# SwiGLU's second products of two token groups: seven block products with a transposed output, woven into the first products, and another order of the groups

## The chip, the cores and the metric

The kernel runs on one core of a Trainium2 chip. The metric is the device time of one execution in microseconds (us). Engines: TensorE (PE; its weight loads are PEld), VectorE (DVE), ScalarE (ACT), GpSimd (POOL) and the sync engine (SP), which issues every DMA of this kernel.

## The reference

Linear attention, a mixture of experts and a SwiGLU block follow each other on 4 x 576 = 2304 tokens of 512 features. The part that the change touches is the last function:

```python
def _moe2_ref(x, w_gate, w_val, w_out, rms_g) -> np.ndarray:
    rms = np.sqrt(np.mean(x * x, axis=-1, keepdims=True) + 1e-06)
    xn = x / rms * rms_g
    g = xn @ w_gate
    silu = g * (1.0 / (1.0 + np.exp(-g)))
    val = xn @ w_val
    return (silu * val @ w_out).astype(np.float32)
```

Here x is 2304 x 512, w_gate and w_val are 512 x 1536, w_out is 1536 x 512. Ahead of it every token goes through all 8 experts (`h = relu(x @ w1[e])`, `h @ w2[e]`, weighted sum). The weights of SwiGLU arrive as 64-bit floats.

## The kernel before

**Tiling.** The tokens are cut into three groups of 512, 896 and 896 (GP = 256, 448, 448, two halves each). The code counts them g = 0, 1, 2; the text calls them the first, second and third group. For each group all experts run first, in units of 256 hidden features (32 units a group, NCH); SwiGLU follows in units of 256 of its 1536 hidden features (6 units a group, NC2). Units are numbered through: 0 to 95 experts, from NU = 96 on SwiGLU. A unit has an "h" part (first products and activation) and a "y" part (second product, added into an accumulator).

**Three matmuls for one.** Every float32 operand is split into a high half (a ScalarE copy) and a low half (a subtraction), and `mm3` (lines 104 to 107) makes three matmuls of each product: high by high, high by low, low by high.

**First products of the large groups.** `seven` (line 792) makes the product of a 2x2-block weight and a 2x2-block x in seven block products instead of eight. Its operands are sums of blocks: those of x are stored in DRAM by the steps of `sx_steps` and loaded into seven tiles by `sx_load` (line 738), those of the weights are prepared in DRAM (`prepare`, line 398) and loaded by `ws_load` (line 287). After each product, ScalarE copies or VectorE adds out of the PSUM banks b1, b2, b3 (lines 801 to 825); line 825 is on GpSimd. SwiGLU runs `seven` twice, for gate and value, so a unit has 14 products. After product i a hook runs what is due there (`task`).

**Second products.** `y_mm` (line 895) takes a tile of 128 tokens as the weights and streams the 512 output columns: 7 token tiles x 2 hidden halves x 3 matmuls in the large groups, 4 x 2 x 3 in the first. Line 1097 adds the tile to the accumulator, and in the last unit line 1103 stores it. Four PSUM banks ("y") take the tiles in turn.

**Output weights.** During the third group's experts the SwiGLU weights are decoded from 64 bits, one step of VectorE or GpSimd at a time (`decode`, `dec`). Gate and value weights go on to `prepare`; the output weights are stored as float32 (W32, lines 360 to 364), and each unit loads its part and splits it (`w2_load`, `w2_split`).

**Order.** Each engine works its instructions in the order in which they are written here, and so does the sync queue: a DMA that waits holds those behind it. `stretch` (line 1140) writes h of unit u ahead of y of unit u - 1. The third group's experts and SwiGLU of the first and second group form one stretch, SwiGLU of the third group another (lines 1146 to 1148). The RMS norm of a group (`norm_steps`: squares, scale, transposes, then storing the x blocks through two pairs of staging buffers) is spread over hooks: the second group's over its successor's experts, the third group's over the SwiGLU units of the other two (lines 1281 to 1286).

## Time and profile before

| | us |
|---|---|
| median of 3 runs (lowest, highest) | 2020.91 (2019.67, 2021.41) |
| profiled execution, its own time | 2020.03 |
| span in the profile | 2018.2 |
| TensorE busy | 1993.7 (99%) |
| VectorE, ScalarE, GpSimd busy | 1407.4, 782.8, 377.5 |
| mean granted clock of TensorE | 0.998 of full speed |

The profile is one execution. A busy time is the time in which an engine had an instruction running; matmuls overlap, so the distance from one start to the next tells what one costs. The SwiGLU stages lie, in us of the span: first group from 1582 to 1687 (with the last expert tiles), second to 1852, third to the end.

### The profile page before, as it was taken

To read this page: it belongs to the slowest core of one execution; us is meant where nothing else is said; L and a number is where in the kernel's file an instruction comes from. 1 tells how busy PE (TensorE), PEld (TensorE's weight loads), DVE (VectorE), ACT (ScalarE), POOL (GpSimd) and SP (SyncE) were. 2 spreads that over 40 slices of the span, in tenths; PEclk is the share of its full clock that TensorE was granted. 3 is DMA by queue.
4 is the path that set the end of the run, shared out by engine and by line. 5 is a ranking of instruction groups with operands and counts; after the bars stand their busy time and mean duration, and the time that the engine had idled before them with its cause. 6 is when DMAs were issued, how large, how long until landed. Compare 5 with 4: busy or idle time off the path is not lost.

```text
span 2018.2 us, 25789 instructions
## 1 busy us (share of the span) xinstructions
PE 1993.7 (99%) x9614; PEld 1715.4 (85%) x9614; DVE 1407.4 (70%) x2161; ACT 782.8 (39%) x1383; POOL 377.5 (19%) x342
## 2 busy tenths in 40 slices
PE   7999999999999999999999999999999999999999
PEld 5777888888888888888888888888888888888887
DVE  8885877776677777776658878878865446565555
ACT  5564333345343343443243333333332253433432
POOL 3320000032222222222022222222220000110100
PEclk9999999999999999999999999999999999999999
DMA  7543322354765555654768778778865647557542
GB/s 203 143 136 110 95 95 100 99 204 177 261 216 199 197 217 211 219 210 172 296 251 285 249 244 312 275 273 286 282 233 195 256 146 263 214 203 276 194 158 74
DMA packets 169853, 415.11 MB, mean 206 GB/s; under 512 B 32256, under 2 KB 81920, under 8 KB 169344
## 3 DMA queue, kind: packets, MB, share of 16 engines
q1 hardware_dynamic: 169728, 413.47, 58.7%
q8 instruction: 75, 1.23, 0.3%
q14 instruction: 50, 0.41, 0.1%
HBM read 281.69 MB, written 131.73 MB: 205 GB/s over the span
## 4 chain that ended last, share of the span: by engine, by line
PE 95%; DVE 3%; ACT 1%; issue 0%; DMA 0%; POOL 0%; DVEq 0%; POOLq 0%; ACTq 0%
PE py L105 13%; PE py L106 13%; PE py L107 13%; PE b_a L107 10%; PE b_a L106 10%; PE b_a L105 10%; PE ph_a L105 3%; PE ph_a L107 3%; PE ph_a L106 3%; PE po L105 2%; PE po L107 2%; PE po L106 2%; PE b_v L105 2%; PE b_v L107 2%; PE b_v L106 2%; PE px L634 1%
## 5 line engine op out<-in xcount | busy, mean ns | idle before, releaser
L105 PE MATMUL py<-w2h,hh 128*128 128x512 f32 x1152 | 452.6, 393 | 0.7 <-ACT lt L684 0.7
L106 PE MATMUL py<-w2l,hh 128*128 128x512 f32 x1152 | 449.0, 390 | 0.0
L107 PE MATMUL py<-w2h,hl 128*128 128x512 f32 x1152 | 448.6, 389 | 0.0
L801 ACT COPY u_a<-b_a 128x448 f32<-128x448 f32 x228 | 121.6, 533 | 692.8 <-PE b_a L107 692.6
L105 PEld LDWEIGHTS py<-w2h,hh 128*128 128x128 f32 x1152 | 216.3, 188 | 47.2 <-issue 1.5
L107 PEld LDWEIGHTS py<-w2h,hl 128*128 128x128 f32 x1152 | 216.3, 188 | 45.7
L106 PEld LDWEIGHTS py<-w2l,hh 128*128 128x128 f32 x1152 | 216.3, 188 | 43.0
L105 PE MATMUL b_a<-sT,wsh_a 128*128 128x448 f32 x608 | 220.0, 362 | 3.2 <-DVE c L815 2.1
L107 PE MATMUL b_a<-sT,wsl_a 128*128 128x448 f32 x608 | 220.6, 363 | 0.0
L106 PE MATMUL b_a<-sT,wsh_a 128*128 128x448 f32 x608 | 220.3, 362 | 0.0
L929 DVE SCALAR_TENSOR_TENSOR slot_a<-py,Pm,slot_a 128x512 f32<-128x512 f32 x217 | 162.6, 749 | 52.3 <-PE py L107 50.4
L929 DVE SCALAR_TENSOR_TENSOR slot_b<-py,Pm,slot_b 128x512 f32<-128x512 f32 x217 | 161.4, 746 | 23.6 <-PE py L107 22.5
L107 PE MATMUL b_a<-sB,wsl_a 128*128 128x448 f32 x456 | 165.7, 363 | 0.3 <-DMA wsl_a<-wdl_a 0.3
L106 PE MATMUL b_a<-sB,wsh_a 128*128 128x448 f32 x456 | 165.2, 362 | 0.0
L105 PE MATMUL b_a<-sB,wsh_a 128*128 128x448 f32 x456 | 165.2, 362 | 0.0
L102 DVE TENSOR_TENSOR w2l<-w2r,w2h 128x512 fp32r<-128x512 f32 x162 | 116.9, 722 | 43.5 <-ACT w2h L101 43.5
L863 DVE SCALAR_TENSOR_TENSOR hl<-c,hh 128x896 fp32r<-128x896 f32 x128 | 143.1, 1118 | 0.9 <-ACT hh L862 0.7
L825 POOL TENSOR_TENSOR c<-u_a,p_a 128x448 f32<-128x448 f32 x64 | 74.2, 1159 | 344.1 <-ACT u_a L801 344.0
L862 ACT ACTIVATE hh<-c 128x896 fp32r<-128x896 f32 x128 | 122.4, 956 | 28.1 <-POOL c L825 28.1
L247 POOL TENSOR_TENSOR sum<-w1r 128x256 f32<-128x256 f32 x32 | 23.8, 742 | 561.5 <-issue 438.1
L101 ACT CAST w2h<-w2r 128x512 fp32r<-128x512 f32 x162 | 97.1, 618 | 81.3 <-PE py L107 77.1
L105 PEld LDWEIGHTS b_a<-sT,wsh_a 128*128 128x128 f32 x608 | 113.7, 187 | 13.1 <-DVE c L815 3.7
(232 smaller groups left out, 3594.9 us busy)
## 6 DMA issues: line engine op xcount, KB each, us to landing
w2r<-in_moe_w_dram SPq DMA_DIRECT2D x96, 512.0 KB, 4.6
w1r<-in_moe_w_dram SPq DMA_DIRECT2D x64, 512.0 KB, 3.4
wsdh<-wsh_a SPq DMA_DIRECT2D x32, 896.0 KB, 6.4
wsdl<-wsl_a SPq DMA_DIRECT2D x32, 896.0 KB, 7.8
wsh_a<-wsdh SPq DMA_DIRECT2D x32, 896.0 KB, 6.8
wsl_a<-wsdl SPq DMA_DIRECT2D x32, 896.0 KB, 8.7
w2d<-w2l SPq DMA_DIRECT2D x32, 512.0 KB, 2.9
w2l<-w2d SPq DMA_DIRECT2D x32, 512.0 KB, 4.8
```

The source lines that it names most:

```text
L101: nc.scalar.copy(hi, src)
L102: (eng or nc.vector).tensor_tensor(lo, src, hi.bitcast(F32), op=ALU.subtract)
L105: nc.tensor.matmul(ps, lh, rh, start=first, stop=False, skip_group_check=True)
L106: nc.tensor.matmul(ps, lh, rl, start=False, stop=False, skip_group_check=True)
L107: nc.tensor.matmul(ps, ll, rh, start=False, stop=last, skip_group_check=True)
L247: nc.gpsimd.tensor_tensor(s1, a21, a22, op=ALU.add)
L634: nc.tensor.matmul(px[:, :H2], st["kv"], st["qT"][:, n], start=True, stop=True)
L801: nc.scalar.copy(tmp[n], bk[i])
L825: nc.gpsimd.tensor_tensor(c[:, 1, 1], tmp["u3"], tmp["p5"], op=ALU.add)
L862: nc.scalar.activation(th, src, AF.Relu)
L863: return lambda: nc.vector.scalar_tensor_tensor(tl, src, 0.0, th.bitcast(F32), op0=ALU.max, op1=ALU.subtract)
L929: nc.vector.scalar_tensor_tensor(a, py, pe, a, op0=ALU.mult, op1=ALU.add)
```

## The change

For the second and third group the second product is also made of seven block products: 2 hidden halves x 2 token halves by 2 hidden halves x 2 output halves. Now the output weights are the stationary operand (128 x 128) and 448 tokens stream, so that the result is transposed: 128 output features by 448 tokens. A unit has 14 tiles of three matmuls.

- `prepare_out` makes the seven blocks of the output weights in DRAM while the other weights are prepared; `wo_load` brings them in four loads a unit, in place of `w2_load` and `w2_split`. `dec` runs the second line of steps on two calls of three, not on every second. W32 is still stored, for the first group.
- `tail_steps` makes the seven hidden blocks (four GpSimd subtractions, seven splits) at the last two hooks of a unit and in the first tiles of the next.
- `y_steps` queues 14 tiles; `y_step` runs one after each block product of the following unit. Each of seven products has its own accumulator, kept over the six units. The first unit copies, later ones add: ten tiles on VectorE from PSUM, four by a ScalarE copy and a GpSimd addition (STAGED).
- `y_end` combines the seven accumulators by seven GpSimd additions; `y_out` turns 32 x 32 blocks on VectorE and stores 32 tokens a DMA.
- The order of SwiGLU becomes second, third, first group. The h parts of the twelve units of the large groups follow each other without y parts between; the last expert tiles come after the first of them.
- The third group's norm moves into five units of the second group, its eight block subtractions (`two`) from VectorE to GpSimd. The loads of the x blocks move to the last expert unit and to the last unit of the second group; the first group's x comes back at unit U0 - 1.

```diff
     LATE = 4
+    TURN2 = (1, 2, 0)
+    U0 = NU + 2 * NC2
     const = ctx.enter_context(tc.tile_pool(name="const", bufs=1))
     slots = ctx.enter_context(tc.tile_pool(name="slots", bufs=1))
...
             del RAW["b", u]
-            if u + 1 < ALL:
-                w2_load(u + 1)
+            n = U0 if u + 1 == NU else u + 1
+            if n < ALL:
+                w2_load(n)
     def ws_alloc(key):
...
@@ -358,10 +361,8 @@
         nc.gpsimd.tensor_tensor(r, r, a.bitcast(F32), op=ALU.add)
         dec_load()
         if kind == "o" and half:
-            r = DEC.pop((kind, c))
             W32[c] = dram.tile([P, KD * CH], F32, tag=f"o{c}", name=f"w32_{c}")
-            nc.sync.dma_start(W32[c], r)
-            LIVE.remove((kind, c))
+            nc.sync.dma_start(W32[c], DEC[kind, c])
     def piece(name):
         return tuple(
...
+    def prepare_out(c):
+        r = DEC.pop(("o", c)).rearrange("p (j i d x) -> p j i d x", j=2, i=4, d=2)
+        d = dram.tile([P, 14 * CH], F32, tag=f"os{c}", name=f"wd_o_{c}")
+        WSD["o", c] = d
+        d = d.rearrange("p (b w n) -> p b w n", b=7, w=2)
+        at = lambda d, j: r[:, j, :, d].rearrange("p i (m b) -> p i m b", m=2)
+        cut = lambda t, n: t[:, n * CH:(n + 1) * CH]
+        by = lambda t, n: cut(t, n).rearrange("p (m i b) -> p i m b", m=2, i=4)
...
+        def put(h, *to):
+            got = []
+            def hi():
+                got.extend(piece(f"o_{c}_{to[0][1]}"))
+                for n, (j, _) in enumerate(to):
+                    nc.scalar.copy(by(got[0], n), at(h, j))
+            def lo():
+                for n, (j, _) in enumerate(to):
+                    nc.vector.tensor_tensor(
+                        by(got[1], n), at(h, j), by(got[0], n).bitcast(F32), op=ALU.subtract
+                    )
+                for n, (_, i) in enumerate(to):
+                    for w, t in enumerate(got):
+                        nc.sync.dma_start(d[:, i, w], cut(t, n).bitcast(F32))
+            return hi, lo
+        a11, a12, a21, a22 = (at(h, j) for h in range(2) for j in range(2))
+        ha, la = put(1, (1, 5))
+        hb, lb = put(0, (0, 0), (1, 2))
+        hc, lc = put(1, (0, 6), (1, 1))
+        hd, ld = put(0, (0, 3), (1, 4))
+        ha()
+        yield
+        la()
+        hb()
+        yield
+        lb()
+        yield
+        nc.gpsimd.tensor_tensor(a22, a21, a22, op=ALU.add)
+        nc.gpsimd.tensor_tensor(a21, a11, a21, op=ALU.subtract)
+        nc.gpsimd.tensor_tensor(a11, a22, a11, op=ALU.subtract)
+        nc.gpsimd.tensor_tensor(a12, a12, a11, op=ALU.subtract)
+        yield
+        yield
+        hc()
+        yield
+        lc()
+        hd()
+        yield
+        ld()
+        LIVE.remove(("o", c))
...
+        if g == NG + 2:
+            two = lambda o, x, y: [
+                lambda: nc.gpsimd.tensor_tensor(o, x, y, op=ALU.subtract)
+            ]
...
-        return (u // NCH, u % NCH) if u < NU else divmod(u - NU, NC2)
+        if u < NU:
+            return divmod(u, NCH)
+        j, c = divmod(u - NU, NC2)
+        return TURN2[j], c
...
-        plain_mm(ph, f, key, stored, range(KD))
+        if YS:
+            for kk in range(KD):
+                plain_mm(ph, f, key, stored, (kk,))
+                y_step()
+        else:
+            plain_mm(ph, f, key, stored, range(KD))
...
+        sg = []
+        mine = tail_steps(u, cg, cv)
+        def later(i):
+            if i == 7:
+                sg.append(gate_sig(flat(cg, 1), 1))
+            elif i == 8:
+                nc.vector.tensor_tensor(flat(cg, 1), flat(cg, 1), sg[0], op=ALU.mult)
+            elif i >= 12:
+                mine.pop(0)()
+            y_step()
+            hook(i)
         hook(-1)
-        seven(("a", u), cg, hook, lambda f: gate_part(flat(cg, f), flat(cg, f), f))
+        seven(("a", u), cg, later, lambda f: f or gate_part(flat(cg, 0), flat(cg, 0), 0))
+        seven(("v", u), cv, lambda i: later(7 + i), lambda f: None)
+        assert not YS
+        YS.extend(y_steps(u, mine))
...
+    STAGED = (0, 5, 8, 12)
...
+    def y_step():
+        if YS:
+            YS.pop(0)()
+    def wo_load(u, i):
+        c = group(u)[1]
+        t = w2p.tile([P, 2, DM], F32R, tag="w2" + "hl"[i % 2], name=f"wo_{u}_{i}")
+        WO[u, i] = t.rearrange("p b (w n) -> p b w n", w=2)
+        n = 2 * DM if i < 3 else DM
+        nc.sync.dma_start(
+            t.rearrange("p b n -> p (b n)")[:, :n].bitcast(F32),
+            WSD["o", c][:, i * 2 * DM:i * 2 * DM + n],
+        )
...
+    def block(u, i, src):
+        tag = "h" + "hl"[i % 2] + "01"[i // 2 % 2]
+        t = hp_.tile([P, 2 * G], F32R, tag=tag, name=f"s_{u}_{i}").rearrange(
+            "p (w n) -> p w n", w=2
+        )
+        SB[u, i] = t
+        split(t[:, 0], t[:, 1], src)
...
+    def tail_steps(u, cg, cv):
+        t1 = cp2.tile([P, G], F32, tag="t1", name=f"t1_{u}")
+        b11, b12, b21, b22 = (cv[:, f, t] for f in range(2) for t in range(2))
+        sub = lambda o, x, y: nc.gpsimd.tensor_tensor(o, x, y, op=ALU.subtract)
...
+        def value(f):
+            nc.vector.tensor_tensor(row(cv, f), row(cv, f), row(cg, f), op=ALU.mult)
+        def s0():
+            value(0)
+            sub(t1, b12, b11)
+            block(u, 0, b11)
+        def s1():
+            block(u, 1, t1)
+        def s2():
+            value(1)
+        def s3():
+            block(u, 2, b21)
+            sub(t1, b22, t1)
+        def s4():
+            block(u, 3, t1)
+            sub(b21, b21, t1)
+        def s5():
+            block(u, 4, b22)
+            sub(b12, b22, b12)
+        return [s0, s1, s2, s3, s4, s5, lambda: block(u, 5, b21), lambda: block(u, 6, b12)]
...
+    def y_steps(u, more_):
+        g, c = group(u)
+        def tile_(p):
+            i, m = divmod(p, 2)
+            if p == 0 and c == 0:
+                ym_place(g)
+            if more_:
+                more_.pop(0)()
+            py = bank("y", G, f"yo_{u}_{p}")
+            w = WO[u, i // 2][:, i % 2, :, m * P:(m + 1) * P]
+            x = SB[u, i]
+            mm3(py, w[:, 0], w[:, 1], x[:, 0], x[:, 1], True, True)
+            a = YM[g][i][:, m * G:(m + 1) * G]
+            if c == 0:
+                if p % 2:
+                    nc.vector.tensor_copy(a, py)
+                else:
+                    nc.scalar.copy(a, py)
+            elif p in STAGED:
+                t = accp.tile([P, G], F32, tag="yt", name=f"yt_{u}_{p}", bufs=2)
+                nc.scalar.copy(t, py)
+                nc.gpsimd.tensor_tensor(a, t, a, op=ALU.add)
             else:
-                fn()
-        seven(("v", u), cv, lambda i: hook(7 + i), after)
+                nc.vector.tensor_tensor(a, py, a, op=ALU.add)
+        return [lambda p=p: tile_(p) for p in range(14)]
...
+    def y_out(g, t, j0, n):
+        a = YM[g]
+        OT.append(OT.pop(0))
+        o = decp.tile([P, DM], F32, tag=OT[0], name=f"yout_{g}_{t}_{j0}", bufs=2)
+        o = o.rearrange("p (j m b) -> p j m b", m=4, b=32)[:, :n]
+        for m in range(4):
+            src = a[((2, 5), (4, 1))[t][m // 2]]
+            c0 = (m % 2) * G + j0 * 32
+            nc.vector.transpose(
+                o[:, :, m], src[:, c0:c0 + n * 32].rearrange("p (j b) -> p j b", b=32)
+            )
+        for j in range(n):
...
+            nc.sync.dma_start(
+                rows[2 * jj + t, p0:p0 + 32, :].rearrange("a (i x) -> i a x", i=4),
+                o[:, j].rearrange("p m b -> p (m b)"),
+            )
...
+    def y_end(g):
+        m = YM[g]
+        add = lambda x, y: (lambda: nc.gpsimd.tensor_tensor(m[x], m[x], m[y], op=ALU.add))
+        steps = [add(2, 0), add(0, 3), add(4, 1), add(4, 0), add(0, 6), add(5, 0), add(1, 0)]
+        return steps + [
+            lambda t=t, j=j: y_out(g, t, j, min(4, G // 32 - j))
+            for t in range(2) for j in range(0, G // 32, 4)
+        ]
...
-    stretch(2 * NCH, NCH + 2 * NC2)
-    stretch(NU + 2 * NC2, NC2)
+    stretch(2 * NCH, NCH)
+    order[-1:] = [("h", NU), order[-1]] + [("h", u) for u in range(NU + 1, U0)]
+    stretch(U0, NC2)
...
-    for u in range(NU, ALL):
+    for u in range(U0, ALL):
         for f in range(2):
-            task("h", u, (0 if group(u)[0] == 0 else 4) + f, lambda u=u, f=f: w2_split(u, f))
+            task("h", u, 5 if u == U0 else f, lambda u=u, f=f: w2_split(u, f))
+    for u in range(NU, U0):
+        for i in range(4):
+            at = ("h", u, min(4 * i + 3, 13))
+            if u == NU:
+                at = ("h", u, i) if i < 2 else ("y", u - 1, 6)
+            task(*at, lambda u=u, i=i: wo_load(u, i))
...
-                if j[0] != "o" and j[2]:
+                if j[2]:
                     PREP.append((j[:2], len(TODO)))
-                LINES[1] = prepare(*PREP.pop(0)[0])
+                kind, c = PREP.pop(0)[0]
+                LINES[1] = prepare_out(c) if kind == "o" else prepare(kind, c)
...
-        if CALLS[0] % 2:
+        if CALLS[0] % 3:
             dec_step(1)
         dec_step(0)
...
-    task("y", NU - 3, 0, first_again)
     for i in range(7):
-        task("h", NU, 0, lambda i=i: sx_load(NG + 1, i))
+        task("h", NU - 1, i, lambda i=i: sx_load(NG + 1, i))
+        task("h", NU + NC2 - 1, 7 + i, lambda i=i: sx_load(NG + 2, i))
     spread(
-        [("y", NU + i // 4, i % 4) for i in range(12)]
-        + [("h", NU + 3 + i // 5, i % 5) for i in range(15)]
-        + [("h", u, i) for u in range(NU + NC2, NU + 2 * NC2 - 1) for i in (0, 1, 3, 4, 7, 9)],
+        [("h", u, i) for u in range(NU + 1, NU + NC2)
+         for i in (0, 1, 3, 6, 7, 7, 8, 9, 10, 10, 11, 12, 13) if u < NU + NC2 - 1 or i < 5],
         lambda: norm_steps(2),
     )
-    for i in range(7):
-        task("h", NU + 2 * NC2 - 1, 7 + i, lambda i=i: sx_load(NG + 2, i))
+    spread(
+        [("h", u, i) for u in range(NU + NC2 + 1, NU + NC2 + 4) for i in (1, 3, 7, 10, 12)],
+        lambda: y_end(1),
+    )
+    task("h", U0 - 1, 0, first_again)
+    spread(
+        [at for u in range(U0 + 1, U0 + 3)
+         for at in [("y", u - 1, i) for i in range(4)] + [("h", u + 1, i) for i in range(6)]],
+        lambda: y_end(2),
+    )
```

## Rows read from the trace of the kernel before

**Rows 1.** The page, part 1: busy time, share of the span, instructions.

```profile
PE 1993.7 (99%) x9614; PEld 1715.4 (85%) x9614; DVE 1407.4 (70%) x2161; ACT 782.8 (39%) x1383; POOL 377.5 (19%) x342
```

**Rows 2.** Waits of TensorE, 1056 us to end: releaser, total us, times, longest.

```profile
PE b_a L105 <- ACT u_a L801: 0.9, 1, 0.9
PE b_a L105 <- DVE c L815: 0.9, 1, 0.9
PE b_a L107 <- DMA wsl_a<-wdl_a: 0.3, 1, 0.3
```

**Rows 3.** Timeline of TensorE: start us, us, engine, line, operation.

```profile
1564.24 0.37 PE L105 MATMUL b_a<-sB,wsh_a 128*128 128x448 f32 x1
...
1572.65 0.39 PE L105 MATMUL py<-w2h,hh 128*128 128x512 f32 x1
...
1593.07 0.39 PE L105 MATMUL py<-w2h,hh 128*128 128x512 f32 x1
...
1602.59 0.39 PE L105 MATMUL ph_a<-slot_a,wsh_a 128*128 128x512 f32 x1
```

**Rows 4.** Groups by form, whole span: xcount, busy us, mean ns, idle before.

```profile
L105 PE MATMUL po<-w2h,hh 128*128 128x512 f32 x216 | 84.4, 391 | 0.0
...
L275 DVE TENSOR_TENSOR wsl_a<-w1r,wsh_a 128x256 fp32r<-128x256 f32 x32 | 13.4, 419 | 0.2 <-ACT wsh_a L271 0.2
```

**Rows 5.** Groups by form of the large groups' SwiGLU, 1687.4 us to end.

```profile
L1049 DVE TENSOR_TENSOR cg<-cv,cg 128x896 f32<-128x896 f32 x24 | 26.2, 1092 | 6.5 <-POOL cv L825 6.1
...
L825 POOL TENSOR_TENSOR cv<-u_v,p_v 128x448 f32<-128x448 f32 x12 | 18.8, 1568 | 90.4 <-ACT u_v L801 83.0 <-DMA wsl_a<-wdl_a 7.5
...
L102 DVE TENSOR_TENSOR w2l<-w2r,w2h 128x512 fp32r<-128x512 f32 x24 | 16.4, 683 | 0.0
...
L825 POOL TENSOR_TENSOR cg<-u_a,p_a 128x448 f32<-128x448 f32 x12 | 15.7, 1310 | 297.6 <-ACT u_a L801 297.6
...
L815 DVE TENSOR_TENSOR cv<-b_v,u_v 128x448 f32<-128x448 f32 x12 | 7.4, 618 | 0.0
...
L390 DVE TENSOR_TENSOR pcl_T<-slot_b,pch_T 128x448 fp32r<-128x448 f32 x8 | 5.0, 623 | 5.0 <-ACT pch_T L387 5.0
```

**Rows 6.** Windows: stretch, length; PE, PEld, DVE, ACT, POOL busy; PEclk, DMA share, GB/s.

```profile
1056.70:1492.40 435.70, 434.68 (x2045) 380.71 (x2044) 356.15 (x568) 157.49 (x270) 121.89 (x104) 1.00 0.79 275
1687.40:1852.30 164.90, 164.90 (x782) 145.74 (x781) 101.51 (x140) 61.47 (x102) 17.32 (x12) 1.00 0.63 233
1840.00:1855.00 15.00, 15.00 (x69) 12.68 (x68) 7.76 (x12) 0.65 (x2) 0.00 (x0) 1.00 1.01 416
1855.00:1870.00 15.00, 14.85 (x74) 13.31 (x72) 7.51 (x11) 6.87 (x12) 1.31 (x1) 1.00 0.68 231
1870.00:1885.00 15.00, 13.88 (x67) 12.41 (x68) 9.43 (x12) 7.26 (x13) 2.87 (x2) 1.00 0.55 203
```

**Rows 7.** Timelines of VectorE, GpSimd and TensorE, 1315 to 1319 us.

```profile
1315.75 1.15 DVE L769 TENSOR_TENSOR slot_a<-slot_a 128x448 f32<-128x448 f32 x1
...
1317.71 0.61 DVE L815 TENSOR_TENSOR c<-b_a,u_a 128x448 f32<-128x448 f32 x1
...
1315.62 0.80 POOL L428 TENSOR_TENSOR dr_v<-dr_v 128x256 f32<-128x256 f32 x1
...
1317.58 0.79 POOL L430 TENSOR_TENSOR dr_v<-dr_v 128x256 f32<-128x256 f32 x1
...
1318.38 0.47 PE L105 MATMUL b_a<-sT,wsh_a 128*128 128x448 f32 x1 [0.91 <-DVE c L815]
```

**Rows 8.** Line 390, tile pcl_v: duration ns min/median/max, first and last start.

```profile
L390 DVE TENSOR_TENSOR pcl_v<-dr_v,pch_v x24: 674/684/1791, 1077.3 to 1481.3; 128x512 fp32r<-128x512 f32 x24
```

**Rows 9.** DMA issues, whole span: xcount, KB each, median us to landing.

```profile
sT<-sdT SPq DMA_DIRECT2D x12, 896.0 KB, 13.7
...
wsh_v<-wdh_v SPq DMA_DIRECT2D x12, 896.0 KB, 4.8
```

**Rows 10.** Timeline of TensorE, its last matmul.

```profile
2013.35 0.39 PE L107 MATMUL po<-w2h,hl 128*128 128x512 f32 x1
```

More of the change, by code (lines that the diff above doesn't have):

```diff
@@ L185, in w2_load @@
         else:
-            nc.sync.dma_start(raw.rearrange("p f d -> p (f d)"), W32[(u - NU) % NC2])
+            nc.sync.dma_start(raw.rearrange("p f d -> p (f d)"), W32[group(u)[1]])
         RAW["b", u] = raw
@@ L294, in ws_load @@
             else:
-                g, c = divmod(key[1] - NU, NC2)
+                g, c = group(key[1])
                 d = WSD[key[0], c, w]
@@ L1072, in unit2_h @@
         cv = cp2.tile([P, 2, 2, G], F32, tag="cv", name=f"cv_{u}")
-        hook(-1)
-        seven(("a", u), cg, hook, lambda f: gate_part(flat(cg, f), flat(cg, f), f))
-        def after(f):
-            fn = value_part(flat(cv, f), flat(cg, f), f)
-            if f:
-                NEXT.append(fn)
-            else:
-                fn()
-        seven(("v", u), cv, lambda i: hook(7 + i), after)
+        sg = []
[9 more added lines that the diff above has]
+            hook(i)
@@ new lines, in unit2_h @@
+        hook(-1)
+        seven(("a", u), cg, later, lambda f: f or gate_part(flat(cg, 0), flat(cg, 0), 0))
+        seven(("v", u), cv, lambda i: later(7 + i), lambda f: None)
+        assert not YS
+        YS.extend(y_steps(u, mine))
+    YS = []
+    YM = {}
+    SB = {}
+    WO = {}
+    STAGED = (0, 5, 8, 12)
+    OT = ["pch", "pcl"]
+    def y_step():
[10 more added lines that the diff above has]
+        )
@@ new lines, in block @@
+    def block(u, i, src):
[9 more added lines that the diff above has]
+        sub = lambda o, x, y: nc.gpsimd.tensor_tensor(o, x, y, op=ALU.subtract)
+        row = lambda t, f: t[:, f].rearrange("p t g -> p (t g)")
+        def value(f):
[18 more added lines that the diff above has]
+        return [s0, s1, s2, s3, s4, s5, lambda: block(u, 5, b21), lambda: block(u, 6, b12)]
@@ new lines, in ym_place @@
+    def ym_place(g):
+        if g == 1:
+            big = slot_a().bitcast(F32)
+            e = slot_e().rearrange("p t d -> p (t d)")
+            more_ = [e[:, 0:2 * G], e[:, 2 * G:4 * G]]
+            x = ["x0", None, None]
+        else:
+            big = slot_b()
+            x = ["x1", "x2", "x0"]
+        more_ = [
+            accp.tile([P, 2 * G], F32, tag=x[n], name=f"ym_{g}_{i}") if x[n] else more_.pop(0)
+            for n, i in enumerate((3, 5, 6))
+        ]
+        four = [big[:, n * 2 * G:(n + 1) * 2 * G] for n in range(4)]
+        YM[g] = four[:3] + [more_[0], four[3], more_[1], more_[2]]
@@ new lines, in y_steps @@
+    def y_steps(u, more_):
[14 more added lines that the diff above has]
+                    nc.vector.tensor_copy(a, py)
+                else:
+                    nc.scalar.copy(a, py)
[3 more added lines that the diff above has]
+                nc.gpsimd.tensor_tensor(a, t, a, op=ALU.add)
+            else:
+                nc.vector.tensor_tensor(a, py, a, op=ALU.add)
+        return [lambda p=p: tile_(p) for p in range(14)]
@@ new lines, in y_out @@
+    def y_out(g, t, j0, n):
[10 more added lines that the diff above has]
+        for j in range(n):
+            b, r = divmod(PB0[g] + (j0 + j) * 32, H2)
+            jj, p0 = divmod(r, SP)
+            rows = out[b * S:(b + 1) * S, :].rearrange("(p c) f -> c p f", c=SC)
+            nc.sync.dma_start(
+                rows[2 * jj + t, p0:p0 + 32, :].rearrange("a (i x) -> i a x", i=4),
+                o[:, j].rearrange("p m b -> p (m b)"),
+            )
@@ L1087, in unit2_y @@
         if c == 0:
-            ACC["o", g] = slot_e() if g == 0 else as_acc(
-                slot_a().bitcast(F32) if g == 1 else slot_b()
-            )
+            ACC["o", g] = slot_e()
         for t in range(TPG[g]):
```

18 lines of the change are left out of this document (9 added, 9 removed).

## The prediction

> **What bounds the kernel now.** I read the page first: TensorE is busy 99% of the span [rows 1], and the chain that ended last is nearly all TensorE. So the time can fall only by what TensorE is given less to do, and it rises by whatever makes TensorE wait. Then its waits: from 1056 us to the end, where all that the change touches lies, it waits three times, 2.1 us in all [rows 2]. Then what one matmul costs, from the starts of neighbours and not from the durations, because they overlap: 42 matmuls of 448 columns run from 1564.24 to 1572.65, 8.41 us, 0.200 each; 42 of 512 columns run from 1593.07 to 1602.59, 9.52 us, 0.2267 each [rows 3]. 64 columns are thus worth 0.0267 us, and the 128x128 weight load costs no more beside 448 columns than beside 512. Last the helpers: VectorE is busy 82% of the third group's expert stretch and 62% of the second group's SwiGLU stretch [rows 6]; GpSimd does 17.3 us in the latter.
>
> **The change part by part.**
>
> *The products.* The second product of a unit of the two large groups is 7 token tiles x 2 x 3 = 42 matmuls of 512 columns; the matmul of line 105 stands 216 times, which is 12 units x 14 + 6 units x 8 [rows 4]. Afterwards it is 7 block products x 2 column tiles x 3 = 42 matmuls of 448 columns, in the shape of the first products. So no matmul disappears; each becomes shorter. 12 x 42 x 0.0267 = 13.4 us fall from TensorE, which has nothing else to do in that time. This is the whole gain.
>
> *Stretch 1, the third group's experts (1056.7 to 1492.4).* prepare_out cuts the output weights into seven blocks: per chunk 7 VectorE subtractions and 7 ScalarE copies of 256 elements and 4 GpSimd additions, all six chunks before SwiGLU starts, the steps on two of three calls instead of every second. A subtraction of 256 takes 0.419 [rows 4], so 42 x 0.42 = 17.6 us more on VectorE, whose 356 of 435.7 us [rows 6] become 374, 86%, or 0.7 us more for each of some 24 units. In one unit it is already late: line 815's addition starts at 1317.71 behind queued work, and TensorE waits 0.91 for it [rows 7]. What hides the new work is the 80 us in which VectorE is idle there. Without that cover all 17.6 us come out at TensorE; if none of it falls ahead of a line-815 addition, nothing does. I take 2.0: VectorE stays below its limit, but a handful of units will wait a few tenths each as the one in rows 7 does. The stores on the sync queue (84 of 128 KB, 11 MB) only join a queue that works at 275 GB/s [rows 6], with loads due more than a unit later.
>
> *Entry into SwiGLU.* The second group now comes first, and its seven x blocks are loaded during the last expert unit. Each block is 896 KB [rows 9] and comes free when one product has read it. The first is free at 1.2 us after that unit's start, the last is needed at 8.4 + 9.5 + 7.2 = 25.1 us. 7 x 0.917 MB, the two halves of the next value weights and two loads of 0.52 MB are 9.3 MB; at the 416 GB/s of 1840 to 1855 [rows 6] that is 22.4 us, so 23.6 plus a landing of some 2. I take 0.5 (0 to 3).
>
> *Inside a SwiGLU unit.* A step is now one block product and one tile, 9 matmuls, 1.8 us; a unit is 14 steps, 25.2 us. VectorE per unit, by rows 5: 6 sums of 0.62, 4 multiplications of 1.09, 7 low halves of 0.62, 10 additions of 0.62 (priced as line 815's) = 18.6 us, 74%. Two weight splits of 0.68 and two low halves of 896 columns go. The sums that hold a PSUM bank have more room than before, because three more matmuls stand behind each product. The tightest new dependence is the first block: value sum, multiplication, ScalarE copy and low half (0.62 + 1.09 + 0.62 + 0.62, with hand-overs some 3.6 us) between product 4 and the tile that follows the next unit's product 0, 5.4 us later. I charge 0.5 for the twelve units (0 to 3). ScalarE's 21 operations of a unit, at VectorE's prices below 15 us, hide there.
>
> *The norm of the third group.* Its 55 steps move out of 18 units into five units of the second group. That adds to VectorE 14 low halves of 0.62 and 7 scales (priced as high), 13 us, 2.6 a unit: 21.2 of 25.2, 84%. GpSimd goes from two operations in a unit (1.3 and 1.6, line 825 [rows 5]) to ten, some 13 us, and two more of the norm's subtractions. Beside GpSimd's additions from 1315.62 on, VectorE's 448-element subtraction took 1.15 [rows 7], where such an operation takes 0.62 [rows 5], and low halves of 0.68 took up to 1.79 [rows 8]: up to 1.1 for one operation. In a unit VectorE has 11 operations with both inputs in SBUF, 15 with the norm's. If none meets GpSimd, nothing is lost; if each loses 0.5, 7.5 us come on top, 28.7 against 25.2, and five units give 17.5 us to VectorE. I take 1.5, nearer to nothing, since GpSimd is idle half the time and a wait below 4.0 us a unit stays hidden. Also queued here are ScalarE copies that wait for a buffer to be stored; behind them stand line 801's copies, for which the products have some 3 us of room.
>
> The Trainium skill, page "SBUF — State Buffer", section "Who interferes with whom", says that a VectorE instruction with two SBUF inputs contends with a GpSimd instruction that reads SBUF, one fully blocking the other. It speaks against this change, which multiplies GpSimd's work beside exactly such instructions; the trace agrees (1.15 for 0.62, while line 815's sum, which reads PSUM, kept its 0.61 beside GpSimd's addition at 1317.58 [rows 7]). By it alone the third rival below would be the forecast.
>
> *Second group to third.* Until now the last two second products, 19 us, stood between the last unit of one group and the first of the next; now the units follow each other, with the tiles inside. From the end of that unit's product 6 the sync queue gets four weight halves and seven x blocks of 0.917 MB and 1.3 MB of output weights, 11.4 MB. At 416 GB/s they need 27.4 us and some 2 to land. The last, the low half of the value weights, is needed 14 steps and 1.0 us later, 26.2. So TensorE waits 3.2. The stall that stands at this place now (0.15 and 1.12 of idle in the windows from 1855 [rows 6], two of the three waits of rows 2) goes, because the next group does not start with two units back to back behind sixteen stores. Net 2.0; at 350 GB/s it would be 8.4 - 1.3 = 7, and with the queue a little ahead -1.
>
> The same page, section "A bandwidth-pool intuition that's wrong (but worth ruling out)", gives about 358 GB/s between HBM and one core. By it the 11.4 MB would take 31.8 us and the sum would be 4.4 us longer. The row shows 416, so the sum goes by the row.
>
> *Ends.* The combination (7 GpSimd additions, 32 VectorE transposes and 28 stores of 64 KB for each group) lies beside later units and is on no path. The first group comes last; its units had no wait where they stood. The kernel still ends with a tile's addition and its stores, 4.9 us after the last matmul's start [rows 10]. 0.
>
> *Sum.* -13.4 + 2.0 + 0.5 + 0.5 + 1.5 + 2.0 = -6.9. The profiled execution took 2020.0, 0.9 under the median of the three runs shown; I set the sum against the median: 2020.9 - 6.9 = 2014.0.
>
> **The rivals.** *All new work hides.* Only the 13.4 go: 2007.5. For it speak idle VectorE and GpSimd in every stretch and that TensorE waited once in 436 us with VectorE at 82%; against it the 27.4 us for 26.2 at the group change. *Loads bound it.* The group change costs 7, the entry 3, and the norm's stores, which add 6.4 MB to a stretch that already draws 218 GB/s (4 x 0.917 and 1.83 MB in 25.2 us), hold ScalarE and so TensorE for 2: 2020.9 - 13.4 + 7 + 3 + 2 + 0.5 = 2020.0. For it: two of the three waits now lie at a group change. Against it: 416 GB/s kept up for 15 us. *GpSimd holds up VectorE* (the other side). In the five units with the norm, VectorE's operations meet GpSimd's; from 4.0 us of such waits a unit VectorE sets the pace. At 0.5 for each of 15 it costs 17.5 instead of 1.5, and stretch 1, where 24 GpSimd additions come on top, 6 instead of 2: 2014.0 + 16 + 4 = 2034; at half of it 2024. For it: rows 7 and 8; against it: VectorE waits only where the two fall together. *The tiles are not shorter* would need 448 columns to cost 0.2267 with these weights; rows 3 exclude it.
>
> **How the numbers follow.** Chances: forecast 0.42, all hidden 0.24, loads 0.16, GpSimd 0.18. Likeliest 2014.0; its own bounds reach 2009 to 2019. The range goes from a little under the second case, 2006.5 (the waits of rows 2 may go as well), to 2027, half-way into the last. About 0.2%, 4.0 us, is what a measurement of this kernel can tell from no change, so faster is below 2016.9. Faster: 0.24 + 0.34 of the forecast's 0.42 = 0.58. Same: its other 0.08 and loads 0.16 = 0.24. Slower: 0.18.
>
> **What would show it.** Spacing of 0.200 in the output tiles, 504 of them in place of 504 of 512 columns; TensorE's waits summing to 8 to 9 us after 1056, the longest at the first units of the third group with a DMA as releaser; VectorE at 84 to 90% in the five norm units. If TensorE waits mostly on VectorE or ScalarE there, the GpSimd rival was right; if DMA waits exceed 8 us, the loads; if all waits stay at 2, the second case. The forecast is wrong if TensorE's busy time does not fall by 13 us.

## The result, and the profile after

The changed kernel takes 2043.6 us (median of 4 runs, 2041.8 to 2048.9); the kernel before took 2020.3 beside it. The ratio is 1.0119, 95% interval 1.0100 to 1.0139: 1.2% slower, where 2014.0 and "faster" were forecast, and outside the range. The profiled execution took 2044.2 us with a span of 2042.4, 24.2 over the span before.

Page of the kernel after, part 1, which answers [rows 1]:

```profile
PE 1992.6 (98%) x9614; PEld 1720.5 (84%) x9614; DVE 1493.7 (73%) x2339; ACT 818.9 (40%) x1501; POOL 560.1 (27%) x476
```

The number of matmuls is the same and TensorE's busy time fell by 1.1 us, not by 13. Does the shorter tile not pay? The timeline of TensorE says it does (start, duration, engine, line, operation):

```profile
1640.95 0.36 PE L107 MATMUL yo<-s,wo 128*128 128x448 f32 x1
1641.15 0.36 PE L108 MATMUL yo<-s,wo 128*128 128x448 f32 x1
1641.36 0.36 PE L109 MATMUL yo<-s,wo 128*128 128x448 f32 x1
1641.56 0.37 PE L107 MATMUL b_a<-sB,wsh_a 128*128 128x448 f32 x1
```

The output tile's matmuls start 0.20 us apart, as forecast. So the 13.4 us were gained, and 37.9 us were lost beside them, as the sum below shows. The first loss is waiting. TensorE's waits from 1056 us to the end, where [rows 2] had 2.1 us in three (releaser, total us, times, longest):

```profile
PE b_a L107 <- DMA sT<-sdT: 7.3, 2, 5.1
PE ph_v L107 <- DMA wsh_v<-wdh_v: 7.2, 1, 7.2
PE ph_a L107 <- DVE w2l L104: 6.3, 1, 6.3
PE b_v L107 <- DVE cg L886: 2.1, 2, 1.3
PE b_a L107 <- DMA sB<-sdB: 1.1, 1, 1.1
PE ph_a L109 <- DMA wsl_a<-wdl_a: 0.8, 1, 0.8
```

The second loss is the larger part of why the busy time did not fall: after each long wait TensorE ran at half clock for some microseconds. The timeline of TensorE around 1990 us:

```profile
1989.21 0.39 PE L109 MATMUL po<-w2h,hl 128*128 128x512 f32 x1
1995.90 0.77 PE L107 MATMUL ph_a<-slot_a,wsh_a 128*128 128x512 f32 x1 [6.30 <-DVE w2l L104]
...
2000.20 0.63 PE L108 MATMUL ph_a<-slot_a,wsh_a 128*128 128x512 f32 x1
2000.62 0.63 PE L109 MATMUL ph_a<-slot_a,wsl_a 128*128 128x512 f32 x1
...
2002.21 0.39 PE L107 MATMUL ph_a<-slot_a,wsh_a 128*128 128x512 f32 x1
2002.44 0.39 PE L108 MATMUL ph_a<-slot_a,wsh_a 128*128 128x512 f32 x1
```

From 1998.5 on the starts are 0.427 apart, the 512 columns of [rows 3] at nearly twice their 0.2267; from 2002.21 they are 0.23 again. Windows of the same kernel (columns as in [rows 6]) show the granted clock with it:

```profile
1580.00:1590.00 10.00, 9.54 (x47) 8.35 (x45) 3.15 (x5) 3.77 (x5) 0.00 (x0) 1.00 1.01 411
1590.00:1600.00 10.00, 8.25 (x33) 7.59 (x34) 3.35 (x4) 2.78 (x6) 1.14 (x1) 0.83 0.72 269
1750.00:1760.00 10.00, 8.76 (x42) 7.27 (x40) 8.56 (x13) 5.13 (x10) 5.30 (x4) 1.00 1.02 420
1760.00:1770.00 10.00, 4.88 (x14) 4.30 (x14) 1.73 (x4) 1.06 (x2) 2.27 (x2) 0.66 0.59 219
1930.00:1940.00 10.00, 6.85 (x31) 5.32 (x29) 7.29 (x6) 1.66 (x3) 9.84 (x5) 1.00 0.04 8
1940.00:1950.00 10.00, 6.00 (x19) 4.40 (x19) 6.23 (x5) 2.59 (x5) 7.33 (x4) 0.66 0.50 178
1990.00:2000.00 10.00, 3.30 (x7) 2.22 (x8) 2.14 (x4) 0.62 (x1) 0.00 (x0) 0.59 0.82 284
```

A mean of 0.59 to 0.83 is a window that held stretches at both levels, 1.2 and 2.4 GHz. Each low one comes with a wait of 2.2 to 7.2 us. Read the DMA columns as well: at the group change (1750 to 1760) the engines are full at 420 GB/s, but at 1930 they are idle at 8 GB/s while TensorE waits for a load. Those are two kinds of wait.

To add it up, take for every pair of neighbouring matmuls the distance of their starts less what the first costs at full clock (0.200 or 0.2267; 0.14 for the norm's transposes). The sums are what TensorE loses to waits and half clock. From 1056 us on they are 6.1 us before and 44.0 after; 44.0 - 6.1 - 13.4 = 24.5, which is the 24.2 measured.

| stretch | lost before | lost after | more | forecast |
|---|---|---|---|---|
| 1, third group's experts, to 1565 | 1.8 | 2.3 | 0.5 | 2.0 |
| entry into SwiGLU, to 1610 | - | 4.1 | 4.1 | 0.5 |
| units of the large groups, the norm in them | 2.7 | 8.0 | 5.3 | 2.0 |
| second group to third (after: 1740 to 1775) | 2.3 | 9.5 | 7.3 | 2.0 |
| first group (before: 1565 to 1687; after: 1910 to the end) | -0.7 | 20.1 | 20.8 | 0 |

(The groups' order changed, so a column's stretches are those with the same work, not the same times.) More than half of the loss sits where the forecast wrote 0, under *Ends*. What is late there is seen on the sync queue (SP), in its timeline of the kernel after:

```profile
1921.73 0.38 SPq L303 DMA_DIRECT2D wsl_a<-wdl_a  x1
1938.76 0.32 SPq L188 DMA_DIRECT2D w2r<-w  x1
1939.19 0.37 SPq L303 DMA_DIRECT2D wsh_v<-wdh_v  x1
...
1973.04 16.37 SPq L1289 DMA_DIRECT2D out_dram<-yout  x20
1989.51 0.55 SPq L188 DMA_DIRECT2D w2r<-w  x1
1990.16 0.38 SPq L303 DMA_DIRECT2D wsh_a<-wdh_a  x1
```

SP issues nothing from 1922.1 to 1938.8: the w2r load stands at its head, its buffer is still read by VectorE's w2 splits, and wsh_v, for which TensorE waits, stands behind it. SP's waits (1915 to 2012) name it: 

```profile
SPq L188 <- DVE w2l L104: 41.7, 4, 16.6
```

The splits stand at the unit's last hook, so they start only at 1933.64, and GpSimd makes them end later still (timelines of VectorE and GpSimd):

```profile
1933.64 5.10 DVE L104 TENSOR_TENSOR w2l<-w2r,w2h 128x512 fp32r<-128x512 f32 x2
...
1933.24 2.46 POOL L1297 TENSOR_TENSOR slot_b<-slot_b,ym 128x896 f32<-128x896 f32 x1
1935.65 5.01 POOL L1297 TENSOR_TENSOR slot_b<-slot_b 128x896 f32<-128x896 f32 x2
```

Two splits take 5.10 us where one took 0.68 [rows 5]: they run beside the combination's additions, seven of them back to back from 1931.0 to 1947.5. That is some 3.7 us of the 16.6; the rest is the place of the load in the queue. The second long wait, at 1989.4, has another cause on the same queue: twenty stores of the combination occupy SP for 16.4 us, and wsh_a is issued behind them. The profile calls VectorE's w2l the releaser there, but the matmul reads wsh_a, which was issued at 1990.16, when TensorE already stood; the label is an event from before that, not the cause.

### The profile page after: what moved, and what is told of

It is laid out like the page before. It is cut to its first block, busy times and chain, and to the rows that moved or that the text cites. A ratio compares the mean times of both kernels' runs of the same rounds, so it can differ in the third digit from the quotient of the medians.

```text
span 2042.4 us, 26562 instructions
## 1 busy us (share of the span) xinstructions
PE 1992.6 (98%) x9614; PEld 1720.5 (84%) x9614; DVE 1493.7 (73%) x2339; ACT 818.9 (40%) x1501; POOL 560.1 (27%) x476
## 4 chain that ended last, share of the span: by engine, by line
PE 85%; DVE 6%; DMA 4%; ACT 2%; POOL 2%; issue 1%; SPq 0%; DVEq 0%; ACTq 0%; POOLq 0%
PE py L107 13%; PE py L108 12%; PE py L109 12%; PE b_a L109 9%; PE b_a L107 9%; PE b_a L108 9%; PE ph_a L107 3%; PE ph_a L109 3%; PE ph_a L108 3%; DMA sT<-sdT 2%; DVE s L104 1%; PE b_v L107 1%; PE b_v L108 1%; PE b_v L109 1%; PE yo L108 1%
## 5 line engine op out<-in xcount | busy, mean ns | idle before, releaser
L104 DVE TENSOR_TENSOR w2l<-w2r,w2h 128x512 fp32r<-128x512 f32 x138 | 107.1, 777 | 49.1 <-ACT w2h L103 49.1
L107 PE MATMUL ph_a<-slot_a,wsh_a 128*128 128x512 f32 x304 | 122.0, 401 | 7.5 <-DVE w2l L104 6.3
```

Source lines behind the costliest of these rows:

```text
L104: (eng or nc.vector).tensor_tensor(lo, src, hi.bitcast(F32), op=ALU.subtract)
L107: nc.tensor.matmul(ps, lh, rh, start=first, stop=False, skip_group_check=True)
```

## The experiments

Five single edits of the changed kernel come first, then versions that put edits together, and last one more single edit.

**1. The stores of the last combination spread out.**

```diff
-        [at for u in range(U0 + 1, U0 + 3)
-         for at in [("y", u - 1, i) for i in range(4)] + [("h", u + 1, i) for i in range(6)]],
+        [("y", U0, i) for i in range(4)] + [("h", U0 + 2, i) for i in range(3)]
+        + [("y", U0 + 1, 0), ("y", U0 + 1, 2), ("h", U0 + 3, 0), ("h", U0 + 3, 3),
+           ("y", U0 + 2, 1), ("h", U0 + 4, 0), ("h", U0 + 4, 3), ("y", U0 + 3, 1)],
```

> Only the places of the third group's eight y_out steps change: they are spread over three units of the first group, the seven GpSimd additions stay where they are. Theory A (28 stores of 0.6 to 0.8 us each, issued in a row on the sync queue, hold the next weights' loads): the wait at 1989.6 of 6.3 and 0.8 us and the 2 us of half clock behind it go, so about 9 us less than the changed kernel's 2043.6, near 2034.5; the 7.15 us wait on wsh_v before it stays. Rival (the split on VectorE, which the wait view names as releaser, is itself late): the wait stays and the time stays within 2 us of 2043.6.

Measured: 2033.2 us, ratio 1.0068 (1.0053 to 1.0083). The second wait and its half clock are gone, the wait for wsh_v stays. Windows:

```profile
1940.00:1950.00 10.00, 5.61 (x13) 4.03 (x14) 5.57 (x4) 2.12 (x4) 7.58 (x4) 0.52 0.51 174
1980.00:1990.00 10.00, 10.00 (x46) 8.29 (x45) 6.05 (x16) 1.84 (x3) 0.00 (x0) 1.00 0.85 246
1990.00:2000.00 10.00, 10.00 (x46) 8.29 (x45) 6.11 (x16) 2.33 (x4) 0.00 (x0) 1.00 0.58 194
```

So the stores ahead of wsh_a on SP are shown to be the cause: moving them (with VectorE's transposes, which took 0.2 to 0.3 us each) gives 10.4 us.

**2. The weight load ahead of the w2 load.** The loop that registers the w2 splits of the first group stands after the one that registers the weight loads, so that at a shared place the load is issued first.

```diff
-    for u in range(U0, ALL):
-        for f in range(2):
-            task("h", u, 5 if u == U0 else f, lambda u=u, f=f: w2_split(u, f))
...
         task("h", u, i, lambda key=key: ws_load(key))
+    for u in range(U0, ALL):
+        for f in range(2):
+            task("h", u, 5 if u == U0 else f, lambda u=u, f=f: w2_split(u, f))
```

> Only the order of two issues on the sync queue changes: at the last hook of unit U0 the value weights of U0 + 1 are loaded ahead of the output weights, whose load waits for VectorE's split. Theory A (in-order sync queue): the 7.15 us wait on wsh_v at 1936.85 and about 2 us of half clock go, near 2034.5. Rival B (GpSimd's additions block VectorE, so that something else of VectorE is late next): the wait moves to a VectorE releaser within the next unit and less than 3 us is gained.

Measured: 2041.2 us, 1.0110 (1.0093 to 1.0127): 2.4 us and not 9. TensorE's waits show a miss of a kind not listed:

```profile
PE ph_a L107 <- DMA wsh_a<-wdh_a: 9.8, 2, 5.7
PE b_a L107 <- DMA sT<-sdT: 7.3, 3, 5.2
```

The wait for wsh_v is gone, but the next unit's gate weights now stand behind the next w2 load and come 4.2 us late (the other 5.7 us are the stores' wait). SP holds that w2 load until VectorE's next splits end, so rival B's bound of 3 us came true, though the name of the releaser did not. Here a blocked head of the queue delayed whatever stood behind it, and taking one load out only changed which.

**3. The last combination's additions on VectorE.**

```diff
-        add = lambda x, y: (lambda: nc.gpsimd.tensor_tensor(m[x], m[x], m[y], op=ALU.add))
+        eng = nc.vector if g == 2 else nc.gpsimd
+        add = lambda x, y: (lambda: eng.tensor_tensor(m[x], m[x], m[y], op=ALU.add))
```

> The third group's seven combining additions run on VectorE instead of GpSimd, same places. If GpSimd's additions of 2.1 us back to back are what makes VectorE's weight splits take 5.1 us for two (0.69 each elsewhere), the splits fall to 0.69, the output-weight load is issued some 4 us earlier, and the 7.15 us wait shrinks to about 3: near 2039. If VectorE's splits are late for another reason, the wait stays at 7 and the time at 2043 or above, with 7.6 us of additions more on VectorE.

Measured: 2038.4 us, 1.0093 (1.0078 to 1.0108), as expected. The two splits (VectorE's timeline) no longer stretch:

```profile
1931.11 1.29 DVE L104 TENSOR_TENSOR w2l<-w2r,w2h 128x512 fp32r<-128x512 f32 x2
```

The wait for wsh_v fell from 7.15 to 3.1 although VectorE got seven operations of 1.09 us more. They do not cost VectorE less there: they take it 7.6 us, and beside GpSimd's additions four splits had taken it 6.9 us longer (9.5 against 2.7). What helps is their place: on VectorE they stand behind these splits, from 1947.3 on, and on GpSimd they ran beside them. The 3.1 us that stay show that the splits' length is only a part of this wait.

**4. The x blocks ahead of the value weights on SP.**

```diff
+    for i in range(7):
+        task("h", NU - 1, i, lambda i=i: sx_load(NG + 1, i))
+        task("h", NU + NC2 - 1, 7 + i, lambda i=i: sx_load(NG + 2, i))
     keys = [("a", u) for u in range(2 * NCH, NU)]
```

(the same three lines are deleted further down)

> At both entries (experts to second group, second to third group) the last x block is loaded ahead of the next value weights instead of behind them. If the issue order decides, the 2.2 us wait at 1589.6 falls to about 1.0 and the 1.08 and 5.12 us at 1754.7 and 1760.1 to about 4.4 together, the rest of it now on wsh_v or wsl_v: 3 to 4 us less in all, near 2040. If only the volume counts, the waits keep their sum and only change their name: 2043.

Measured: 2039.1 us, 1.0094 (1.0079 to 1.0109). At the entry 2.2 us of waiting became 0.46; at the change 6.35 became 3.76. Part of the change's wait is thus order, the rest is volume.

**5. Fewer bytes at the change.** The second group's last unit loads no output weights and uses those of the unit before.

```diff
+        if u == NU + NC2 - 1:
+            WO[u, i] = WO[u - 1, i]
+            return
         t = w2p.tile([P, 2, DM], F32R, tag="w2" + "hl"[i % 2], name=f"wo_{u}_{i}")
```

> The changed kernel, except that the second group's last unit loads no output weights and uses those of the unit before, so its result is not the reference's. 1.3 MB of the 11.4 MB behind product 6 go, 3.1 us at 416 GB/s. If the volume sets the wait at the change to the third group (1.08, 0.15 and 5.12 us), it falls from 6.3 to about 3. If something else does (a block freed late, VectorE), it stays above 5.

Measured in one run: 2038.3 us; the waits at the change 6.35 -> 3.25. 1.3 MB less took 3.1 us off, which is 1.3 MB at 420 GB/s: in this order of issues the volume sets the wait, as the forecast's term for the change said.

**6. The queue mended:** edits 1 and 4, and all w2 splits of the first group at place 5, behind the weight loads.

```diff
+            task("h", u, 5, lambda u=u, f=f: w2_split(u, f))
```

> The changed kernel with its stores spread (as e1), the x blocks ahead of the weights (as e4), and in the first group every output-weight split at the unit's last hook, behind the loads of the gate and value weights on the sync queue. Theory A: the order of issues made the waits of 7.15, 6.3 and 0.8 us and most of the entry's; they go with the half clock behind them. TensorE then waits some 7 us after 1056 (3.6 at the change from the second to the third group, 1.3 and 1.4 on VectorE, 0.5 at the entry) and the time is near 2020, 23 us under the changed kernel. Rival B (GpSimd's combining additions hold VectorE up): new waits of 3 us or more on VectorE or ScalarE appear from 1930 to 1950 and the time stays above 2025.

Measured: 2018.7 us (10 runs, 2016.3 to 2020.9), 0.9994 (0.9984 to 1.0003): no difference from before. All long waits are gone, 24.9 us were won back, and the 13.4 still don't show. What is left from 1556 us on:

```profile
PE b_v L109 <- DMA wsl_v<-wdl_v: 3.9, 4, 1.5
PE b_v L107 <- DVE cg L886: 2.1, 2, 1.3
PE b_a L107 <- ACT s L103: 1.0, 1, 1.0
PE b_a L107 <- DMA sT<-sdT: 0.8, 1, 0.8
```

By the table's method TensorE loses 21.1 us here, 15 more than before: many small pieces, and the units of the large groups hold 10.3 of them. The first group's stage, which lost 20.1, loses 0.8. Yet its two splits are as long as before beside GpSimd's additions (VectorE's timeline):

```profile
1929.69 5.14 DVE L104 TENSOR_TENSOR w2l<-w2r,w2h 128x512 fp32r<-128x512 f32 x2
```

So it was the order of the queue that made TensorE wait; GpSimd only made that wait longer.

**7 and 8. The tiles ahead.** In the second group's last unit the tiles follow its products as one block, to give the loads time, and the first SwiGLU unit starts behind the last expert tiles (8: with edit 3 as well).

```diff
-    order[-1:] = [("h", NU), order[-1]] + [("h", u) for u in range(NU + 1, U0)]
+    order.extend(("h", u) for u in range(NU, U0))
...
+        if u == LAST1:
+            for p in range(14):
+                y_step()
```

> As m1, and the loads at the two entries get more time: the last expert tiles come ahead of the first SwiGLU unit again, and in the second group's last unit the 14 output tiles stand in one block behind its products (its last three hooks and its output-weight loads with them). By the working that sets bytes against time (11.4 MB at 416 GB/s), the 3.6 us at the group change and the 0.5 us at the entry go: near 2016, TensorE waiting some 4 us after 1056. If the loads there are slower than 416 GB/s, 2 us and more remain: 2018.

> As m2, with the third group's combining additions on VectorE. If GpSimd's additions still cost something in the first group's stage, 1 to 2 us less than m2; if the queue order was all, the same within 1 us.

Measured: 2019.1 us, 0.9997 (0.9988 to 1.0006), and 2020.7, 1.0004 (0.9994 to 1.0014). The waits for loads at entry and change are gone but for 0.4 us (8), and others came in their place, in 7 ScalarE's u_a (1.9) and VectorE's cg (2.6) the longest. Both expectations missed: it was no longer the loads that bound the stage, and the two runs cannot be told apart.

**9. Entry and places:** experiment 6 with the entry's order of 7, and the second group's combination moved so that no store stands ahead of a value-weight load.

```diff
-         for i in (1, 3, 7, 10, 12)],
+         for i in (0, 1, 4, 8, 9)],
         lambda: y_end(1),
```

> Builds on the kernel with the queue mended (2018.7), whose remaining TensorE waits after 1056 us sum to 9.5 us in pieces of 0.2 to 1.5. Two of them are taken away alone: the first SwiGLU unit's products stand behind the last expert tiles (its value weights came 0.65 late), and the second group's combination and stores stand at other places of their units, so that no store stands ahead of a value-weight load on the sync queue (1.52 and 0.22 at 1867.8 and 1841.8). Theory A (each small wait is a head-of-line wait on its own queue, independent of the others): those 2.4 us are gone and nothing takes their place, 2016.3. Theory B (the stage is short of something as a whole, and a wait taken away comes back at the next release, as when the tiles were put ahead): 2018 to 2019.

Measured: 2021.5 us, 1.0009 (1.0000 to 1.0018). Theory A fell, and the time lies above theory B's too. The waits for wsl_v went from 3.9 to 1.5, and those for VectorE's cg (line 886) from 2.1 to 6.3.

**10. The gate later:** 9 with the first sigmoid multiplication behind the last addition.

```diff
-            if i == 7:
-                sg.append(gate_sig(flat(cg, 1), 1))
+            if i in (5, 7):
+                sg.append(gate_sig(flat(cg, i // 7), i // 7))
+            elif i == 6:
+                nc.vector.tensor_tensor(flat(cg, 0), flat(cg, 0), sg[0], op=ALU.mult)
...
-        seven(("a", u), cg, later, lambda f: f or gate_part(flat(cg, 0), flat(cg, 0), 0))
+        seven(("a", u), cg, later, lambda f: None)
```

> The one before, and the gate's first sigmoid multiplication stands behind the last addition of the seven products instead of ahead of it on VectorE (before: 2.45 us at 1814.87 where it takes 1.09 alone, with the addition that TensorE waited for 1.29 us behind it). Theory A (VectorE is late there because a multiplication from SBUF stretched beside GpSimd stands ahead of the addition): the two waits of 0.83 and 1.29 us on that addition go, 2 us less than the kernel before it, 2014.3. Theory B (VectorE has too much work in the unit, and its place does not matter): the wait moves to the value product's additions or to a block half, within 0.5 us of the kernel before it.

Measured: 2018.9 us, 0.9996 (0.9987 to 1.0004). The 6.3 us on cg became 0.2 and the time gained 2.6, which is theory A's difference; its 2014.3 had taken experiment 9 to reach 2016.3. It only got back to experiment 6. In this profile VectorE itself waits for GpSimd, see the next.

**11. No tile on GpSimd:** 10 with `STAGED = ()`.

```diff
-    STAGED = (0, 5, 8, 12)
+    STAGED = ()
```

> The one before, with all 14 output tiles of a unit added by VectorE (four of them went through ScalarE and GpSimd): GpSimd loses four additions of 1.2 to 2 us a unit, VectorE gains four of 0.61. Theory A (GpSimd's additions stretch VectorE's operations from SBUF): the block halves come down from 1.0 to 1.9 us towards 0.61, VectorE's busy time in 1690 to 1740 (43.6 of 50 us) does not rise, and the time is within 1 us of the kernel before it or less. Theory B (VectorE's own number of operations is the limit): its busy time rises by about 1.2 us a unit and TensorE waits for it more, 2 us or more slower than the kernel before it.

Measured: 2012.2 us (5 runs, 2011.6 to 2014.2), 0.9961 (0.9948 to 0.9975). It beats both kernels; before took 2019.5 beside it, so that 7.3 of the 13.4 us now show. The window 1640 to 1740, and then groups by form from 1640 to 1892 (the gate's fourth block on GpSimd; the value product and the block halves on VectorE), of experiment 10:

```profile
1640.00:1740.00 100.00, 96.93 (x486) 87.79 (x485) 80.86 (x118) 52.22 (x103) 59.69 (x44) 1.00 0.78 272
```

```profile
L887 POOL TENSOR_TENSOR cg<-u_a,p_a 128x448 f32<-128x448 f32 x9 | 15.0, 1666 | 1.1 <-ACT u_a L863 1.1
...
L1202 DVE TENSOR_TENSOR cv<-cv,cg 128x896 f32<-128x896 f32 x18 | 21.4, 1189 | 4.2 <-POOL cv L887 4.2
...
L104 DVE TENSOR_TENSOR s<-cv,s 128x448 fp32r<-128x448 f32 x49 | 43.3, 884 | 16.2 <-ACT s L103 16.2
```

The same of experiment 11:

```profile
1640.00:1740.00 100.00, 98.68 (x497) 90.52 (x496) 89.98 (x133) 47.38 (x90) 39.38 (x31) 1.00 0.84 283
```

```profile
L887 POOL TENSOR_TENSOR cg<-u_a,p_a 128x448 f32<-128x448 f32 x10 | 12.2, 1220 | 43.6 <-ACT u_a L863 43.6
...
L1202 DVE TENSOR_TENSOR cv<-cv,cg 128x896 f32<-128x896 f32 x18 | 22.2, 1233 | 0.0
...
L104 DVE TENSOR_TENSOR s<-cv,s 128x448 fp32r<-128x448 f32 x48 | 40.8, 850 | 14.3 <-ACT s L103 14.0
```

Neither theory holds as written. VectorE's busy time rose, from 80.9 to 90.0 of 100 us (B), and yet TensorE waits less (A's outcome). The block halves hardly got shorter (0.884 to 0.850), so a stretched VectorE operation is not the main thing. What changed is GpSimd's queue: in 10 the engine was idle for 1.1 us in all ahead of nine of the gate's fourth blocks, so they came up behind other work; in 11 it stood idle for 43.6 ahead of ten, so each starts as soon as its data is there and takes 1.22 instead of 1.67, and VectorE's value product no longer waits 4.2 us for GpSimd. That this is worth all of the 6.7 us is argued, not shown: the edit also takes away ScalarE's copies (two waits of TensorE for its u_v, 1.4 us, are among those that went) and some meetings of the two engines. And the two profiled executions, 2017.6 and 2014.2 us, lie 3.4 apart, so the traces hold half of it.

**12. The same edit alone on the changed kernel.**

> The changed kernel with one edit: all 14 output tiles of a unit are added by VectorE, none by ScalarE and GpSimd. On the kernel with the queue mended this edit was worth 6.7 us. Theory A (GpSimd's four additions hold up the units themselves, whatever the loads do): the same 5 to 7 us here, 2037 to 2039. Theory B (they cost only where the loads do not bound the stage, since the long waits of the changed kernel, 2.2, 6.4, 7.2 and 7.1 us, give the late engines time to catch up): 2 us or less, 2042 to 2044.

Measured: 2042.3 us, 1.0111 (1.0094 to 1.0128): 1.3 us, which cannot be told from none. The time is theory B's, but its reason does not fit the trace. In the second group's units (1610 to 1740) TensorE loses 2.5 us instead of 4.8 by the table's method, much as from experiment 10 to 11 (5.2 to 2.6). In the first group it loses 2.2 more, where the wait for wsh_v grew from 7.15 to 8.6. So the gain in the units came here too and was spent again at the blocked queue; that is one trace of each kernel.

## Why the prediction was wrong

*The products* were right: 504 matmuls of 448 columns at 0.20, 13.4 us less at full clock. The last sentence, that the busy time must fall by 13 us, was wrong as a test: busy time counts a matmul at half clock at its longer duration.

*Ends* is the step that failed. It put the combination beside later units and "on no path", and said of the first group's units that they "had no wait where they stood". It priced the operations and not the queues they join. Each of the first group's units at the end loads four weight halves and a w2 block over the same SP that issues 28 stores of 0.54 to 1.93 us each, and its w2 splits share VectorE with 32 transposes and run against 7 GpSimd additions. 7.15, 6.3 and 0.8 us of waiting, 0.7 of smaller pieces and 4.7 nearly all at half clock, against 0. Experiment 1 shows the stores, 2 and 6 the blocked head of the queue, 3 the additions' share. With the order mended in 6 the stage loses 0.8, with the additions still on GpSimd.

*Unpriced: the clock.* No term said what a wait costs beyond itself. The distances between 0.08 and 0.45 us over full price sum to 12.6 us after and 3.8 before; some 8.7 of the 12.6 lie behind the four long waits, at half clock.

*Entry*: 0.5 forecast, its bound 3, 4.1 measured, 2.4 of waiting and 1.5 at half clock. The bound had the bytes right (424 GB/s in 1570 to 1580) and left out that the last needed x block was issued behind value weights that are needed later; experiment 4 shows that order.

*Second group to third*: 3.2 of waiting forecast, 6.35 measured, 3.76 in the better order, the half clock on top. The volume was right (experiment 5) and the place in the queue wrong: the prediction took the value weights' low half for the last to come, and it was an x block, needed earlier, that stood behind them. The Trainium skill's 358 GB/s, weighed there, did not hold (420 and 417 GB/s over 10 us); its page "Perfetto Trace Analysis", section "Roofline", says that a core alone can draw more than that share, and the trace agrees.

*Inside the units, and the norm*: 2.0 forecast, 5.3 measured. The direction was right, and the way was partly another: not only that VectorE's operations get longer beside GpSimd, but also, as experiment 11 suggests, that GpSimd's own queue of ten operations a unit makes the fourth block late. VectorE was not short of time as a whole: 81% busy in the five norm units (1610 to 1740), under the 84 to 90% that were forecast. *Stretch 1* was overpriced: 0.5 for 2.0. VectorE was busy for 364 of its 435.7 us and not 374, and TensorE's two waits there, 0.6 and 0.3 us, were for ScalarE.

*The rivals.* "Loads bound it" named two right places and its test (DMA waits above 8 us) came true, but its 2020 held nothing for the end. "GpSimd holds up VectorE" was the one on the right side, with 2034; its mechanism is seen at 1933 us, in a stage for which it was not considered. The Trainium skill, "SBUF — State Buffer", "Who interferes with whom", says that a VectorE operation with two SBUF inputs contends with a GpSimd instruction that reads SBUF, and calls the port pair that they share an exclusive lock. The trace agrees: 2.55 us per split beside additions of 2.1 to 2.5, for 0.68 alone.

## What to carry to other kernels

When work moves, write down the issue order of each in-order queue it joins, the DMA queue first, and ask of each entry what it waits for and who stands behind it; cheap work off the path is paid for by the load behind it. On a kernel that keeps TensorE full, price a long wait together with the half clock that may follow: four waits of 2.2 to 7.2 us brought some 8.7 us more here. And when mending one wait only brings out the next, look for an engine that is late everywhere by a little: with the queue mended, taking away four of GpSimd's ten operations in a unit won 6.7 us, and experiments 7 to 9, which rearranged loads and stores, won nothing.

## What was not expected of the hardware

The clock: after waits of 2.2, 5.1, 7.2 and 6.3 us TensorE's matmuls stood for some 3 to 6 us at 0.373 (448 columns) and 0.427 us (512). In all runs every wait of 3.9 us or more, from 1056 us on, went with a granted clock at half. Of the shorter ones some did: 1.5 us in experiment 6, 1.9 in 5 and 12, 2.3 in 1, 2.6 in 8, 3.1 in 3. Others of the same lengths did not: 1.5 in 9, 2.0 in 2, 2.3 in 3, 2.6 in 7, 3.25 in 5. So between 1.5 and 3.3 us the length of a wait does not tell. Windows with the 2.63 us of experiment 8, the 2.64 of 7 and the 3.25 of 5 (columns as in [rows 6]):

```profile
1730.00:1740.00 10.00, 7.52 (x31) 6.92 (x32) 4.77 (x6) 2.52 (x5) 1.15 (x1) 0.83 0.99 401
1730.00:1740.00 10.00, 7.36 (x37) 6.29 (x36) 6.17 (x8) 4.18 (x7) 1.15 (x1) 1.00 0.96 356
1755.00:1765.00 10.00, 6.75 (x34) 5.99 (x34) 6.78 (x10) 4.00 (x7) 2.31 (x2) 1.00 0.73 273
```

The stores: a 64 KB store of the combination holds SP for 0.53 to 2.23 us, 0.61 in the middle:

```profile
L1289 SPq DMA_DIRECT2D out_dram<-yout x56: 529/606/2225, 1827.4 to 1988.7; - x56
```

while a value-weight half of 896 KB took 0.42 in the middle, so that in this kernel the number of transfers, not their bytes, fills that queue.
